# Group 1's channels with exchanged halves: x of both groups in eight 32x64 float32 tiles, weights summed on TensorE, own buffers for the last five stores

## The chip, the core and the metric

The kernel runs on one core of a Trainium2 chip. The metric is the device time of one launch in microseconds (us). The core has five engines that each work through their own list of instructions in order: TensorE (PE in the profile, PEld its weight loads), VectorE (DVE), ScalarE (ACT), GpSimd (POOL) and SyncE (SP), which here issues every DMA. They wait for each other through semaphores. TensorE writes into PSUM, a small memory of eight banks (512 float32 per partition each); all other tiles lie in SBUF.

## The reference

Two attentions and a gated convolution, in numpy, with B = 8 batches, H = 8 heads, S = 576 positions, D = 64, 32 packed queries, and 512 channels (H times D):

```python
def sm_attn(qq, kk, vv):
    s = scale * np.matmul(qq, kk.transpose(0, 1, 3, 2))
    s = s - np.max(s, axis=-1, keepdims=True)
    a = np.exp(s)
    a = a / (np.sum(a, axis=-1, keepdims=True) + 1e-09)
    return np.matmul(a, vv)
p_packed = sm_attn(p, k, v)                 # 32 rows per head
x = sm_attn(q, p_packed, p_packed)          # then heads side by side: B, S, 512
...
for k in range(K):                          # K = 5 taps, causal, per channel
    gate_pre += conv_w[k][None, None, :] * xp[:, k:k + S, :]
gate = 1.0 / (1.0 + np.exp(-gate_pre))
val = x @ w_val
return (gate * val @ w_out).astype(np.float32)
```

The three weights `w_val`, `conv_w` and `w_out` arrive as float64, all else as float32.

## The kernel before

The work is done batch by batch, with heads in two groups g of four (hl = 0 to 3; each has 32 rows of a 128-partition tile). Channels come in four chunks of 128, two per group, so a chunk is two heads.

A batch runs through these steps, each a generator with a letter. Loads K, V, Q, P. `keys` (k) and `queries` (q) turn the loaded tiles by TensorE transposes (tiles `kpt`, `qpt`) that ACT copies to `kT`, `qT`. `attn_pack` (a, lines 343 to 387) makes the first attention: scores `s`, maximum `nb` on DVE, exponential `a` on ACT, transposes `at`, products `pv`, and from these the packed values: `ppd` (each head's 64 values twice, ACT) and `pp` (the same with a mask of zeros, DVE). `packed_turned` (p) turns `ppd` into `ppT`. `attn_out` (s) and `weighted` (t) make the second attention's weights: scores, 32x32 transposes into `t` on DVE, subtraction and scaling on POOL, exponential on ACT, transposes into `a2`; then `a2h`, its rounding to float32r on ACT, and `a2l`, the rest, on DVE. Float32r takes one pass through TensorE, and a product of two split numbers takes three float32r matmuls. `packed_values` (w) multiplies the packed values with `w_val` (`wp`, split into `wph` and `wpl`), so that `value` (v, line 523) needs 12 float32r matmuls per chunk, of `a2h` and `a2l` with these (`val`).

`mixed` (x, line 463) makes x itself, for the convolution. The matrix of a pair of heads has 64 rows and 128 columns, half of them the mask's zeros; `pp` is split into `pph` (ACT) and `ppl` (POOL), and for each group and each half of the positions (288 columns) six float32r matmuls, three for each pair, fill one PSUM tile of two banks, one bank per pair. ACT copies it to `xp`. `gate` (g, line 503) does the five taps per chunk (one on ACT, four on DVE, tile `sig`) and a tanh on ACT. In `value`, DVE multiplies gate and value (`sig<-sig,val`), ACT rounds to `gvh`, POOL takes the rest `gvl`. `project` (o, line 576) multiplies these with `w_out` in 12 float32r matmuls of 512 columns per 128 positions; ACT copies the sum to `osb` (two buffers) and SP stores it. For the last batch five such sums (c = 4 to 8) are held in PSUM until the last chunk of values is there.

The weights come first, once: each tile of 128x512 float64 is loaded as pairs of 32-bit words (tile `words`, five buffers), turned into a float32 `top` and a small `rest` by bit operations (`from_double`, line 240), and added on POOL: to `wv` (W, line 267), `cw` (C), and, split in two, `woh` and `wol` (O, line 289).

The PSUM tiles of two banks have the tag `big`, with two buffers: scores of both attentions, `wp`, x, `val` and one of the last sums share them. The tag `mid` has three buffers of one bank, `out` one.

The order of everything is a table written out in the kernel (`ORDER`, line 49): each token, as `v3.2`, runs the generator `value` of batch 3 for two of its steps. Engines do what they are given in that order, each waiting for its own inputs. The tag of a tile in a name is followed by batch, group or chunk: `x_3_1_0` is batch 3, group 1, half 0, `val_2_3` batch 2, chunk 3. The program's instructions are all issued from a helper, so the profile shows line 94 for each of them; names tell them apart.

Of the kernel before, what the change touches and what calls it, by code (L numbers as in the profile page):

```python
# [9 lines left out]
F32 = mybir.dt.float32  # L10
# [18 lines left out]
 'pp': 2,  # L29
 'ppd': 1,  # L30
 'ppT': 2,
 'pph': 1,
 'ppl': 1,
# [21 lines left out]
q1 t0 q1 g0 t0 w1 O0 g0 q1.2 w1 O0 q1.2 s1 O0 k2 q1 O0 s1 q1 K2 k2.2 V2 O0 s1 q1 Q2 k2.2 V2 k2 Q2 s1 K3 a2 P4 O0
s1.2 a2 s1 a2 k2 g0 k2.2 s1 g0 t0 v0 k2 g0 s1 t1 k2 s1 x0 v0 t1 k2 k3 | v0 a2 g0 x0 q2 k3 a2 v0 x0 q2 t1 q2 a2.3
x0 g0 v0 a2 q2 g0 x1 t1 x1 a2 q2 a2 t1 a2 q2.2 g0 a2.2 q2 t1 g0 x1 q2 g0 x1 v0 t1 a2 k3 q2 a2 x1 K3 x1 a2 V3 k3
g0 k3 Q3 v0 q2 P5 t1 k3.2 v0 q2 a2 t1 v0 k3 g0 a2 x1 t1 a2.3 g0 k3 a2.2 k3 g0 k3 a2.2 g0 p2 a3 g0 v0 p2 g0 k3.2
s2 v0 a3 k3 k4 v0 s2 a3 q3 s2 a3 q3 V3 g0 Q3 v0 K4 k4 a3 s2 K4 P6 a3.2 g0 a3 q3 s2 w2 g0 a3 q3 t2 g0 x1 a3 q3
a3.2 w2 v0 t2 a3.2 w2 v0 s2 q3 v0 g1 t2 o0 a3.2 t2 a3 g1 t2 s2 v1 o0 g1 s2 a3 g1 q3 a3.2 s2 x1 q3 o0 a3 Q4 o0 V4  # L60
x1 g1 s2 g1 t2 g1 v1 a3 t2 o0 k4 a3.2 o0 v1 g1 x1 k4 V4 t2 a3 v1 p3 x1 v1 a3 p3 t2 g1 x2 s3 t2 g1 q3 k4 s3 x2
q3.2 k4 o0 g1 q3 Q4 s3 g1 x2 g1 s3 v1.2 g1 q4 s3 k4 v1 q4.2 o0 K5 s3 k4 o0 q4 g1 k4 a4 s3 k4.2 g1 v1 k4 s3 g1 o0
a4 s3 g1.2 v1 a4 g1 s3 g1 v1 x2 o0 q4 g1 x2.2 o0 v1 q4 Q5 q4 x2 v1 q4 g1.2 x2.2 t3 g2 k4 v1 t3 x2 q4 K5 k4 k5 x2
v1 P7 g2 a4 q4 t3 x2 v1 o1 k5 a4 t3 x3 g2 a4.2 x3 t3 a4 o1 k5 t3 a4.2 o1 v2 k5 a4 g2 t3 a4 o1 a4 g2 t3 g2.2 v2
t3 q4 g2 v2 k5 Q5 t3 a4 q4 k5 g2 k5 o1 V5 w3 a4.2 v2 o1 k5 a4 K6 a4 k5 g2 a4.2 w3 o1 g2 k5 w3 a4 x3 g2.3 v2 o1
g2 o1 g2 o1 v2 g2 v2 g2 v2 g2 v2 o1 g2 o1 k5 g2 a4 x3 k5 v2 a4.2 g2 x3.2 v2 g2 V5 k5 a4 x3 a4 p4 v2 a5 K6 k5 p4
v2 g2 a5 x3 g3 a5 g3 o1 v2 g3 v2 g3 a5 v2 o1 v3 o1 a5 g3 a5 o2 a5 g3.2 v3 g3 v3 g3 a5 o2 k6 s4 v3 a5 o2 k6 x3 s4
q5 x3 a5 g3 x3 q5 a5 v3 s4 x3 g3 x4 s4 g3 a5 q5 g3 v3 o2 x4 s4 x4 g3 a5 q5 v3 t4 v3 a5 o2 s4 o2 a5.2 t4 V6 a5.2
q5 s4 a5.2 v3 q5 Q6 g3 a5 t4 g3 q5 t4 a5 s4 k6 q5 a5 w4 g3 k6 t4 g3 q5 k6 s4 g3 v3 a5 k6 w4 g3 x4 V6 o2 v3 g3 s4
w4 v3 x4 a5 q5 a5 t4 p5 o2 k6 g3 p5 q5 o2 k6.2 q5 t4 x4 Q6 k6 K7 s5 x4 g3 k6 s5 v3 g3 x4 t4 g4 k6 s5 t4 a6 g4 k6  # L70
v3 s5 q6 k6 K7 o2 a6 q6 v3 g4 s5 t4 a6 g4 t5 a6 o2 s5 o2 v3 a6 o3 s5 a6 t5 a6 s5 g4 t5 s5 g4 v4 g4 s5 g4 a6 o3
# [39 lines left out]
def packed_attention_gated_conv(  # L111
# [69 lines left out]
    for hl in range(4):  # L181
        nc.gpsimd.memset(mask[heads[hl], hl % 2, :], 1.0)
# [31 lines left out]

    def words_of(nm, src, rows):
# [442 lines left out]
```

## Time and profile before

| what | us |
|---|---|
| median of 3 runs (lowest, highest) | 329.72 (329.62, 330.51) |
| the profiled execution's own time | 330.79 |
| its span, first to last instruction | 329.0 |
| PE busy | 287.6 |
| DVE busy | 259.0 |
| ACT busy | 215.3 |
| POOL busy | 123.2 |

An engine's busy time is the union of its instructions' times. Matmuls overlap in the array, so the pace of TensorE is read from one start to the next and not from durations: 12 matmuls of `o` take 2.75 us, though each lasts about 0.39. In a row of the timeline the columns are the start, the duration, the engine, the instruction, the tiles as out<-in, their shapes, and in brackets the idle time before it with what ended it; "x16" is sixteen records merged (a float32 matmul leaves two).

### The profile page before, as it was taken

Reading aid. Unit: us, or ns where it says so; the run is one execution under the profiler, and the core shown is the slowest. Engines: PE = TensorE matmul, PEld = TensorE weight load, DVE = VectorE, ACT = ScalarE, POOL = GpSimd, SP = SyncE. Lnnn points to the kernel's source line nnn. Section 1 sums busy time; section 2 is a strip of 40 time slices with the busy share of each in tenths; the row PEclk is TensorE's granted clock in tenths of the full one; section 3 lists DMA queues with packets and bytes.
Section 4 is the critical chain, followed back from the end, with each engine's and each line's share of the span. In section 5 each row is a group of like instructions: output and inputs, shape, how many; then the busy total and the mean of one; then the engine's idle time right before and its main releaser. Section 6 shows DMA issues by size and latency. Waiting matters only on the chain.

```text
span 329.0 us, 7252 instructions
## 1 busy us (share of the span) xinstructions
PE 287.6 (87%) x2932; PEld 220.6 (67%) x2932; DVE 259.0 (79%) x381; ACT 215.3 (65%) x440; POOL 123.2 (37%) x115
## 2 busy tenths in 40 slices
PE   0157987979989999999999898989999999999990
PEld 0134744657758877877877677776868868778870
DVE  0794288689999999997797999998997899776600
ACT  0347788779986779777686867776677755655201
POOL 1334536374153455323245434415431237323200
PEclk9999997699999999999999999999999999999996
DMA  7999989495895765383507491635011011211013
GB/s 197 232 255 263 257 162 239 108 230 108 211 217 135 187 166 136 90 241 92 157 34 173 118 237 37 175 87 126 32 66 34 32 35 38 70 53 64 34 24 135
DMA packets 42474, 43.47 MB, mean 132 GB/s; under 512 B 6085, under 2 KB 36805, under 8 KB 42442
## 3 DMA queue, kind: packets, MB, share of 16 engines
q1 hardware_dynamic: 42442, 43.02, 53.6%
q8 instruction: 23, 0.38, 0.5%
q14 instruction: 9, 0.07, 0.1%
HBM read 33.57 MB, written 9.44 MB: 131 GB/s over the span
## 4 chain that ended last, share of the span: by engine, by line
PE 40%; DVE 31%; ACT 17%; issue 4%; DMA 3%; POOL 3%; SPq 1%; ACTq 0%; POOLq 0%
DVE sig L94 16%; PE o L94 15%; PE val L94 8%; ACT sig L94 4%; DVE a2l L94 3%; PE x L94 3%; PE s L94 3%; PE kpt L94 3%; PE pv L94 2%; DVE sm L94 2%; PE at L94 2%; DVE t L94 2%; DVE nb L94 2%; DMA wv_words<-in_moe_w_val_dram 2%; PE qpt L94 2%
## 5 line engine op out<-in xcount | busy, mean ns | idle before, releaser
L94 DVE SCALAR_TENSOR_TENSOR sig<-xp,cw,sig 128x576 f32<-128x576 f32 x128 | 122.6, 958 | 11.6 <-ACT sig L94 10.1
L94 POOL TENSOR_TENSOR gvl<-sig,gvh 128x576 fp32r<-128x576 f32 x31 | 49.1, 1584 | 80.0 <-ACT gvh L94 77.0
L94 PE MATMUL o<-woh,gvh 128*128 128x512 f32 x144 | 58.6, 407 | 0.8 <-ACT osb L94 0.8
L94 PE MATMUL o<-woh,gvl 128*128 128x512 f32 x144 | 56.5, 392 | 0.1
L94 PE MATMUL o<-wol,gvh 128*128 128x512 f32 x144 | 56.5, 392 | 0.0
L94 PE MATMUL val<-a2h,wph 128*128 128x288 f32 x128 | 39.6, 309 | 0.5 <-ACT a L94 0.5
L94 PE MATMUL val<-a2l,wph 128*128 128x288 f32 x128 | 37.9, 296 | 0.9 <-DVE a2l L94 0.9
L94 ACT COPY osb<-o 128x512 f32<-128x512 f32 x34 | 19.8, 582 | 28.3 <-PE o L94 22.6
L94 PE MATMUL val<-a2h,wpl 128*128 128x288 f32 x128 | 37.9, 296 | 0.0
L94 PEld LDWEIGHTS o<-woh,gvh 128*128 128x128 f32 x144 | 27.0, 188 | 10.3 <-issue 2.3
L94 ACT CAST gvh<-sig 128x576 fp32r<-128x576 f32 x32 | 21.7, 678 | 17.7 <-DVE sig L94 17.6
L94 POOL TENSOR_TENSOR t<-t,mx 128x576 f32<-128x576 f32 x16 | 24.2, 1513 | 22.0 <-DVE mx L94 22.0
L94 PEld LDWEIGHTS o<-woh,gvl 128*128 128x128 f32 x144 | 27.1, 188 | 6.6 <-POOL gvl L94 0.5
L94 ACT ACTIVATE sig<-sig 128x576 f32<-128x576 f32 x32 | 21.9, 686 | 13.1 <-DVE sig L94 12.9
L94 PEld LDWEIGHTS o<-wol,gvh 128*128 128x128 f32 x144 | 27.1, 188 | 4.6
L94 POOL TENSOR_TENSOR t<-t,rs 128x576 f32<-128x576 f32 x16 | 20.0, 1248 | 23.0 <-DVE rs L94 15.8
L94 DVE SCALAR_TENSOR_TENSOR sig<-sig,val 128x576 f32<-128x576 f32 x32 | 23.7, 741 | 5.6 <-PE val L94 3.0
L94 PE MATMUL qpt<-ident,qm 96*128 96x96 f32 x192 | 26.1, 270 | 1.1 <-ACT kT L94 1.1
L94 PE MATMUL kpt<-ident,km 96*128 96x96 f32 x192 | 26.8, 276 | 0.1
L94 PEld LDWEIGHTS val<-a2h,wph 128*128 128x128 f32 x128 | 24.2, 189 | 3.6 <-ACT a L94 1.2
L94 PEld LDWEIGHTS qpt<-ident,qm 96*128 96x128 f32 x192 | 21.0, 155 | 7.3 <-issue 4.3
L94 PEld LDWEIGHTS kpt<-ident,km 96*128 96x128 f32 x192 | 20.9, 156 | 6.9 <-issue 4.7
(87 smaller groups left out, 561.8 us busy)
## 6 DMA issues: line engine op xcount, KB each, us to landing
km<-in_k_dram SPq DMA_DIRECT2D x16, 576.0 KB, 7.4
vm<-in_v_dram SPq DMA_DIRECT2D x16, 576.0 KB, 6.1
qm<-in_q_dram SPq DMA_DIRECT2D x16, 576.0 KB, 6.0
out_dram<-osb SPq DMA_DIRECT2D x24, 256.0 KB, 2.2
wv_words<-in_moe_w_val_dram SPq DMA_DIRECT2D x8, 256.0 KB, 7.2
wo_words<-in_moe_w_out_dram SPq DMA_DIRECT2D x4, 512.0 KB, 10.0
out_dram<-osb SPq DMA_DIRECT2D x8, 192.0 KB, 2.3
p<-in_p_dram SPq DMA_DIRECT2D x16, 64.0 KB, 9.0
```

Of the source, the lines that this page charges most:

```text
L94: made = getattr(self.engine, op)(*args, **kw)
```

## The change

**x (`mixed`).** `pp`, its mask, `pph` and `ppl` go. Each head is a tile of its own: 32 rows (its packed positions) by 64 columns (its channels), in plain float32, from `ppd` and `a2` directly. Both groups of a half are issued together, eight matmuls into two `big` tiles, and ACT copies the two afterwards. Head hl of group g writes partitions 0 to 63 or 64 to 127, by (hl + g) mod 2. In group 1 the two heads of a chunk therefore stand in exchanged halves, so that the eight tiles cover all four positions of 32 rows and both of 64 columns.

**Channels.** To match, the chunks of group 1 have exchanged halves everywhere: the loads of `w_out` and `conv_w` fetch them so, and `wv`'s columns are exchanged in the copy.

**Weights.** TensorE adds `top` and `rest`: two float32 matmuls with the identity into one PSUM bank (tag `mid`). `wv` is then copied by ACT in two pieces; `woh` is ACT's rounding of half of the sum, and `wol` one DVE operation on the sum. The `rest` of `w_out`, before an ACT and a POOL operation, is a DVE operation, as it was for `w_val`. For each tile of `w_out` POOL loses three operations, ACT two, and DVE has two more; for each of `w_val` POOL loses one and ACT has two more.

**Last stores.** The five last sums get buffers of their own: two of `osb`, two of `t2`'s, one of `a2`'s.

**Order.** The table is written anew.

```diff
+def summed(nm, words):
+    ps = one(f"{nm}_sum")
+    pe.matmul(ps, ident, st["top", nm], start=True, stop=False)
+    pe.matmul(ps, ident, words[:, :, 0].bitcast(F32), start=False, stop=True)
+    return ps
 def value_weights(b):
...
-            pool.tensor_tensor(
-                wv[:, c, :], st["top", f"wv{c}"], words[:, :, 0].bitcast(F32), op=ALU.add
-            )
+            ps = summed(f"wv{c}", words)
+            yield
+            for low in range(2):
+                cs = slice(low * DM // 2, low * DM // 2 + DM // 2)
+                to, x = (
+                    y[:, cs].rearrange("a (x t d) -> a x t d", x=2, t=2) for y in (wv[:, c], ps)
+                )
+                act.copy(to[:, :, ::-1] if low else to, x)
+                yield
 def out_weights(b):
...
-            yield from from_double(f"wo{c}", words, P, 0.5, True)
-            top, hi = st["top", f"wo{c}"], woh[:, c, :]
-            act.mul(top, top, 0.5)
-            yield
-            act.copy(hi, top)
-            yield
-            pool.tensor_tensor(top, top, hi.bitcast(F32), op=ALU.subtract)
-            yield
-            pool.tensor_tensor(wol[:, c, :], top, words[:, :, 0].bitcast(F32), op=ALU.add)
+            yield from from_double(f"wo{c}", words, P)
+            ps, hi = summed(f"wo{c}", words), woh[:, c, :]
+            yield
+            act.mul(hi, ps, 0.5)
+            yield
+            dve.scalar_tensor_tensor(
+                wol[:, c, :], ps, 0.5, hi.bitcast(F32), op0=ALU.mult, op1=ALU.subtract
+            )
             yield
 def attn_pack(b):
...
-            dve.scalar_tensor_tensor(pp[:, g], pv2, rs, mask, op0=ALU.mult, op1=ALU.mult)
 def mixed(b):
...
+        for half in range(2):
+            hc = slice(half * HS, half * HS + HS)
+            pp, a2 = st["ppd", b], st["a2", b]
+            xps = [big(f"x_{b}_{g}_{half}") for g in range(G)]
+            for g in range(G):
+                for hl in range(4):
+                    at = D * ((hl + g) % 2)
+                    pe.matmul(
+                        xps[g][at : at + D, hl // 2, :HS],
+                        pp[heads[hl], g, 0, :],
+                        a2[heads[hl], g, hc],
+                        start=True,
+                        stop=True,
+                    )
+            yield
+            for g in range(G):
+                act.copy(st["xp", b, g][:, :, half, PAD:], xps[g][:, :, :HS])
                 yield
 def project(b):
...
+            if b == B - 1 and c % 2:
+                osb = tile_of("t2", [P, G, NBLK, NP], F32, f"osb_{b}_{c}")
+                osb = osb.rearrange("a g y z -> a (g y z)")[:, :DM]
+            elif b == B - 1 and c == 8:
+                osb = tile_of("a2", [P, G, S], F32, f"osb_{b}_{c}")[:, 0, :DM]
+            else:
+                osb = tile_of("osb", [P, DM], F32, f"osb_{b}_{c}")
 ORDER (start)
-K0 L0.3 V0 P0 W0.13 L0 W0 L0 W0 L0 Q0 W0 K0 W0 k0 P1 W0 k0.4 W0 k0.2 W0 C0 W0 k0 C0 a0 W0 C0 W0 a0 W0 a0 q0 C0
+x0 K0 x0 L0 Q0 L0 P0 W0.9 q0 K0 W0 V0 q0.2 W0 V0 q0.2 Q0 W0 q0 L0 W0.2 L0 W0.2 L0 k0.11 a0 k0.2 a0 k0 a0.15 q0
```

How the table moves instructions shows at three places. TensorE at the program's start, before (`pTt` turns the packed queries, `qpt` and `kpt` a third of a group's queries or keys):

```order
L94 MATMUL pTt_0_131<-ident_64,p_0_97 128x128 x2
L94 MATMUL kpt_0_0_0_141<-ident_64,km_0_0_84 128x96 x4
L94 MATMUL kpt_0_0_1_147<-ident_64,km_0_0_84 128x96 x4
L94 MATMUL kpt_0_0_2_155<-ident_64,km_0_0_84 128x96 x4
L94 MATMUL s1_0_0_166<-kT_0_0_140,pT_0_138 32x288 x8
```

and now (`wv0_sum` and `wv1_sum` are the first two tiles of `w_val`):

```order
L89 MATMUL wv0_sum_101<-wv0_top_95,ident_64 128x512
L89 MATMUL wv0_sum_101<-wv0_words_84,ident_64 128x512
L89 MATMUL qpt_0_0_0_109<-ident_64,qm_0_0_87 128x96 x4
L89 MATMUL qpt_0_0_1_120<-ident_64,qm_0_0_87 128x96 x4
L89 MATMUL qpt_0_0_2_129<-ident_64,qm_0_0_87 128x96 x4
L89 MATMUL wv1_sum_142<-wv1_top_106,ident_64 128x512
L89 MATMUL wv1_sum_142<-wv1_words_89,ident_64 128x512
L89 MATMUL pTt_0_154<-ident_64,p_0_92 128x128 x2
```

Two sums and a third of the queries now stand ahead of the first transposes of keys and of `s1_0_0`, the first scores.

ScalarE at the program's start, before:

```order
L94 ACTIVATE wv0_top_100<-wv0_words_86 128x512
L94 ACTIVATE wv1_top_107<-wv1_words_89 128x512
L94 ACTIVATE wv2_top_114<-wv2_words_92 128x512
L94 ACTIVATE pT_0_138<-pTt_0_131 128x256
L94 COPY kT_0_0_140<-kpt_0_0_0_141 128x4x96
```

and now:

```order
L89 ACTIVATE wv0_top_95<-wv0_words_84 128x512
L89 COPY wv_71<-wv0_sum_101 128x256
L89 COPY wv_71<-wv0_sum_101 128x2x2x64
L89 ACTIVATE wv1_top_106<-wv1_words_89 128x512
L89 COPY qT_0_0_108<-qpt_0_0_0_109 128x4x96
```

The two copies of the first sum now stand ahead of `wv1_top`, the first step of the second tile.

TensorE around batch 3's x, before (first half, then what follows up to the second half's end):

```order
L94 MATMUL x_3_0_0_2047<-a2h_3_1727,pph_3_1796 128x288 x2
L94 MATMUL x_3_0_0_2047<-a2h_3_1727,ppl_3_1797 128x288 x2
L94 MATMUL x_3_0_0_2047<-a2l_3_1728,pph_3_1796 128x288 x2
L94 MATMUL pv_4_1_2057<-vm_4_1_1472,a1t_4_1_1941 32x64 x24
L94 MATMUL x_3_0_1_2084<-a2h_3_1727,pph_3_1796 128x288 x2
L94 MATMUL x_3_0_1_2084<-a2h_3_1727,ppl_3_1797 128x288 x2
L94 MATMUL x_3_0_1_2084<-a2l_3_1728,pph_3_1796 128x288 x2
```

and now, around the second half:

```order
L89 MATMUL val_2_3_2056<-a2h_2_1302,wph_2_1332 128x288
L89 MATMUL val_2_3_2056<-a2h_2_1302,wpl_2_1333 128x288
L89 MATMUL val_2_3_2056<-a2l_2_1303,wph_2_1332 128x288
L89 MATMUL x_3_0_1_2075<-a2_3_1822,ppd_3_1296 64x288 x4
L89 MATMUL x_3_1_1_2076<-a2_3_1822,ppd_3_1296 64x288 x4
L89 MATMUL ppTt_4_2086<-ident_64,ppd_4_1803 128x128 x2
```

The second half of both groups stands right behind the last matmuls of `val_2_3`, which fill the other `big` tile; the rows before have one group each, with other work between.

More of the change, by code (lines that the diff above doesn't have):

```diff
@@ L28 @@
  'pT': 1,
- 'pp': 2,
- 'ppd': 1,
+ 'ppd': 2,
  'ppT': 2,
- 'pph': 1,
- 'ppl': 1,
  'qT': 2,
@@ L55 @@
[L55 to L59, printed above, removed]
@@ L177, in packed_attention_gated_conv @@
     heads = [slice(NP * hl, NP * hl + NP) for hl in range(4)]
-    pairs = [slice(2 * NP * pr, 2 * NP * pr + 2 * NP) for pr in range(2)]
-    mask = const.tile([P, 2, D], F32, name="mask")
-    nc.gpsimd.memset(mask, 0.0)
-    for hl in range(4):
-        nc.gpsimd.memset(mask[heads[hl], hl % 2, :], 1.0)
     eps = const.tile([P, G * NBLK], F32, name="eps")
```

113 lines of the change are left out of this document (46 added, 67 removed).

## Prediction

> **What bounds the kernel now.** I read the page first: the engines' shares and the chain that ended last.
>
> ```profile
> span 329.0 us, 7252 instructions
> PE 287.6 (87%) x2932; PEld 220.6 (67%) x2932; DVE 259.0 (79%) x381; ACT 215.3 (65%) x440; POOL 123.2 (37%) x115
> PE 40%; DVE 31%; ACT 17%; issue 4%; DMA 3%; POOL 3%; SPq 1%; ACTq 0%; POOLq 0%
> ```
>
> TensorE is busy longest and DVE is second, and both are on the chain, so no single engine sets the time everywhere. The busy time by stretches tells where each does. Its columns are the stretch, its length, and the busy time of PE, PEld, DVE, ACT and POOL, each with its number of instructions; then the granted clock.
>
> ```profile
> core 0: us, PE busy (x) PEld busy (x) DVE busy (x) ACT busy (x) POOL busy (x), PEclk, DMA share, GB/s
> 0.00:44.00 44.00, 22.50 (x247) 15.36 (x248) 22.01 (x39) 21.19 (x45) 15.37 (x25) 1.00 1.04 240
> 44.00:72.00 28.00, 23.07 (x297) 14.88 (x298) 22.57 (x37) 22.98 (x51) 15.08 (x13) 0.82 0.84 176
> 72.00:100.00 28.00, 26.39 (x399) 19.52 (x398) 26.18 (x46) 25.47 (x58) 12.35 (x12) 1.00 0.86 182
> 100.00:180.00 80.00, 79.80 (x819) 63.22 (x818) 71.93 (x104) 57.91 (x122) 30.81 (x27) 1.00 0.53 140
> 180.00:260.00 80.00, 76.31 (x823) 58.99 (x822) 72.65 (x104) 58.62 (x118) 28.72 (x26) 1.00 0.39 100
> 260.00:307.00 47.00, 45.75 (x299) 37.62 (x298) 39.87 (x50) 26.05 (x45) 20.88 (x16) 1.00 0.14 46
> 321.00:329.00 8.00, 0.00 (x0) 0.00 (x0) 0.69 (x1) 1.17 (x2) 0.00 (x0) 0.65 0.37 132
> ```
>
> There are three parts. Up to 72 nothing is full: PE is idle for 21.5 of the first 44 us and for 4.9 of the next 28, DVE for 22.0 and 5.4, so the length of batch 0's chain counts. From 100 to 180 PE has no gap (79.80 of 80); from 180 to 307 PE and DVE are both near full, and wait for each other. In the last 8 us no matmul runs at all.
>
> **The change part by part.** *The last stores.* The timeline's end, with ACT's copies of the sums:
>
> ```profile
> 317.63 0.39 PE L94 MATMUL o<-woh,gvl 128*128 128x512 f32 x1
> ...
> 318.06 0.59 ACT L94 COPY osb<-o 128x512 f32<-128x512 f32 x1 [7.92 <-PE o L94]
> ...
> 320.35 0.39 PE L94 MATMUL o<-woh,gvl 128*128 128x512 f32 x1
> 321.72 0.58 ACT L94 COPY osb<-o 128x512 f32<-128x512 f32 x1 [3.07 <-DMA out_dram<-osb]
> ...
> 324.83 0.59 ACT L94 COPY osb<-o 128x512 f32<-128x512 f32 x1 [2.53 <-DMA out_dram<-osb]
> ```
>
> The first sum ends at 317.63 + 0.39 = 318.02 and is copied 0.04 later. The last ends at 320.74, but its copy waits for a store to free one of two buffers and starts at 324.83. With five buffers it starts at 320.78: **-4.0**. What is late next is the last matmul itself; the stores stay in line on SP, but each is short. This gain needs only that PE's end stays where it is relative to the rest.
>
> *x on TensorE.* One half of one group, six float32r matmuls, and behind it a set of eight float32 score tiles (64 rows by 32 columns each, 288 positions, side by side in the array):
>
> ```profile
> 238.37 0.40 PE L94 MATMUL x<-a2h,pph 64*128 64x288 f32 x2
> ...
> 238.96 0.72 PE L94 MATMUL s<-kT,pT 64*32 64x288 f32 x16
> ...
> 239.61 0.55 PE L94 MATMUL kpt<-ident,km 96*128 96x96 f32 x4
> ```
>
> From start to start, x's half takes 238.96 - 238.37 = 0.59 and the scores' set 0.65. The new half of both groups is also eight float32 tiles of 288 positions, only of another shape; I take the scores' 0.65. If the eight didn't run side by side at all, each would take about a set's time, 8 x 0.65 = 5.2; below 0.65 I see no way, since as many positions stream through. In batches 1 to 7 PE then does 14 x 0.65 = 9.1 in place of 28 x 0.59 = 16.5: 7.4 less.
>
> *What x took on the other engines.*
>
> ```profile
> L94 DVE SCALAR_TENSOR_TENSOR pp<-pv,sm,mask 128x128 f32<-128x128 f32 x16 | 5.4, 338 | 7.3 <-ACT ppd L94 7.2
> L94 POOL TENSOR_TENSOR ppl<-pp,pph 128x256 fp32r<-128x256 f32 x8 | 7.1, 894 | 5.5 <-ACT pph L94 4.6 <-POOL gvl L94 0.9
> L94 DVE SCALAR_TENSOR_TENSOR sig<-xp,cw,sig 128x576 f32<-128x576 f32 x128 | 122.6, 958 | 11.6 <-ACT sig L94 10.1
> L94 DVE SCALAR_TENSOR_TENSOR sig<-xp,cw,sig x128: 718/818/2069, 58.7 to 307.1; 128x576 f32<-128x576 f32 x128
> ```
>
> DVE loses `pp`, 14 x 0.338 = 4.7 in batches 1 to 7. It also loses collisions with POOL: the gate's operation has a median of 818 ns, a mean of 958 and up to 2069, an excess of 128 x 0.14 = 17.9 us over POOL's 123.2 busy us, or 0.145 per us of POOL; `ppl`'s 7.1 are worth 1.0. DVE has 5.7 less. Where PE and DVE wait for each other, I count the smaller of 7.4 and 5.7: **-5.7** (between -7.4 and 0, if the new order leaves the room as gaps).
>
> *Two big buffers at once.* x now fills both `big` buffers, so it waits for the reader of the tile filled just before, not of the one before that. PE is in order: everything behind x waits too. The readers:
>
> ```profile
> L94 DVE SCALAR_TENSOR_TENSOR sig<-sig,val 128x576 f32<-128x576 f32 x32 | 23.7, 741 | 5.6 <-PE val L94 3.0 <-ACT sig L94 2.3
> L94 ACT COPY xp<-x 128x576 f32<-128x576 f32 x32 | 20.6, 644 | 2.8 <-PE x L94 2.5
> L94 ACT CAST wph<-wp 128x1024 fp32r<-128x1024 f32 x8 | 8.1, 1013 | 2.2 <-PE wp L94 2.2
> L94 DVE TENSOR_TENSOR wpl<-wp,wph 128x1024 fp32r<-128x1024 f32 x8 | 9.8, 1220 | 1.9 <-ACT wph L94 1.8
> ```
>
> In the new order eight of the 14 halves of batches 1 to 7 have under 1 us of PE work between the tile filled last and themselves. Four have 0.2 or none: two right behind a `val` chunk (batch 3, as quoted, and batch 7: 0.74 to wait each), one behind `wp_5` (1.01 + 1.22 - 0.2 = 2.0), one behind its own first half in batch 6 (2 x 0.644 - 0.2 = 1.1); a fifth, in batch 1, has 0.7 against such copies (0.6). That is 5.2; I take two thirds, **+3.5**, since PE isn't the late one at each. It is nothing where PE would have waited anyway, and 14 x 1.29 = 18 if every half waited for two copies; the others have 0.7 to 3 us of transposes, products or `o` as cover.
>
> *The weights.* A sum is two float32 matmuls of 512 columns. Nearest is the set of eight float32 `wp` matmuls of 512 columns, side by side:
>
> ```profile
> 41.38 1.96 PE L94 MATMUL wp<-wv,ppT 64*32 64x512 f32 x16
> 141.20 1.09 PE L94 MATMUL wp<-wv,ppT 64*32 64x512 f32 x16
> 142.22 0.42 PE L94 MATMUL at<-ident,a 128*96 128x128 f32 x2
> L94 PE MATMUL o<-woh,gvl 128*128 128x512 f32 x144 | 56.5, 392 | 0.1
> L94 DVE SCALAR_TENSOR_TENSOR wv_top<-wv_top,wv_words 128x512 uint32<-128x512 uint32 x4 | 5.5, 1378 | 0.3
> L94 DVE SCALAR_TENSOR_TENSOR wo_top<-wo_top,wo_words 128x512 uint32<-128x512 uint32 x4 | 2.7, 674 | 0.1
> ```
>
> The set takes 1.02 from start to start at 141 and 1.96 at 41; one matmul alone can't take longer, nor less than a float32r pass (0.392). I take 0.9, so 1.8 a sum and 14.4 for eight (6.3 to 31). Three (w_val's) fall into the first 44 us, where PE's 21.5 idle cover them; five, 9.0, come in 44 to 100, where PE is idle for 4.9 + 1.6: 2.5 stay uncovered. DVE gets eight operations more, 8 x 0.674 = 5.4, under its 5.4 + 1.8 idle in the same stretch. POOL's additions of w_val go, beside which `wv_top` took 1378 ns in place of 674: 4 x 0.70 = 2.8 less on DVE, of which I count 1.0, since DVE often waits there. Opening: **+1.5**. The first product `val`, which came at 69.62,
>
> ```profile
> 69.62 0.40 PE L94 MATMUL val<-a2h,wph 128*128 128x288 f32 x1 [0.49 <-ACT a L94]
> ```
>
> now stands behind fewer instructions, but transposes of batch 2 that were ahead of it come behind it: moved, not saved, and I count nothing. ACT's changes (`pph` gone, eight small copies more) lie in its idle time, 9 to 45% of each stretch from 44 on.
>
> The sum: -4.0 - 5.7 + 3.5 + 1.5 = -4.7. The profiled execution took 330.79, 1.8 more than its span of 329.0, and 1.1 more than the median of 329.72; -4.7 makes its span 324.3 and the median **325.0**. A difference of 0.3%, 1.0 us, is about the least that a measurement here can tell.
>
> **The rivals.** *A: tiles that share a bank (slower).* In the present kernel, whatever runs side by side on different rows writes to different PSUM banks: the pairs of x, the halves of the scores, the groups of `wp`. In the new x, heads 0 and 1 (and 2 and 3) of a group sit on different rows and write one bank, though other partitions. If such tiles took turns, a half would take two rounds, 1.3, and PE 16 x 0.65 = 10.4 more: 325.0 + 10.4 = 335.4. It decides the sign from 0.65 + 4.7/16 = 0.94 a half. No row here shows two row tiles in one bank, for or against; the different partitions speak against it. Chance 0.12. The Trainium skill, TensorEngine Tiling (Array Packing), section Gotcha 1: PSUM Pressure, says that "Different row tiles cannot access same PSUM bank simultaneously"; by that rule the time is this rival's.
>
> *B: the opening comes later (slower).* ACT takes `wv1_top` only after the first sum and its copies, and PE turns the first keys only after two sums.
>
> ```profile
> 9.91 0.69 ACT L94 ACTIVATE wv_top<-wv_words 128x512 f32<-128x512 f32 x1 [0.28 <-DMA wv_words<-in_moe_w_val_dram]
> 15.10 0.66 PE L94 MATMUL pTt<-ident,p 128*128 128x128 f32 x2 [15.10 <-DMA p<-in_p_dram]
> 21.04 1.22 PE L94 MATMUL s<-kT,pT 64*32 64x288 f32 x16 [3.36 <-ACT kT L94]
> ```
>
> With sums of 3.9 and copies of some 0.4, `wv1_top` moves from 9.91 to about 16.7, and the first scores, behind the second sum, from 21.04 to about 27.7: +6.7, if nothing of it is won back by the shorter way from there: 331.7. For it: `pTt` at 15.10 had been waiting for a load. Against: PE's idle 21.5. Chance 0.13.
>
> *C: the opening comes sooner.*
>
> ```profile
> 26.31 2.18 PE L94 MATMUL kpt<-ident,km 96*128 96x96 f32 x12
> 65.47 1.06 PE L94 MATMUL kpt<-ident,km 96*128 96x96 f32 x8
> ```
>
> At 26 a transpose takes 0.18, at 65 0.13, and the `wp` set took 1.96 at 41: early PE works at a slower pace, though the granted clock reads 1.00. If the long sums bring the full pace from 16 us on, PE's 22.5 busy us in the first 44 shrink by up to half, 11; about half of this would lie on batch 0's chain: -6, so 319. Chance 0.17. The Trainium skill, TensorE: Matmul & The Clock Gate, Part 1, says that the array runs at half clock until about 3.4 us of sustained activity; by that rule a first sum is nearly enough, and the pace in these rows agrees, the granted clock doesn't.
>
> *D: only the stores.* DVE's count of operations stays (-5.4 `pp`, +5.4 weights), and if DVE's order sets the middle, PE's room becomes gaps: 329.72 - 4.0 = 325.7. For it: PE 76.31 of 80 beside DVE 72.65. Chance 0.10.
>
> **How the numbers follow.** My forecast has 0.48. Faster by over 0.3% (below 328.7): 0.85 of it, C, 0.8 of D: 0.66, rounded to 0.65. Slower (above 330.7): A, 0.8 of B and a little of the forecast's own spread: 0.25. Within: 0.10. The range takes in B and C and leaves A out, with 1.5 beyond both for the unknown sums and waits: 317.5 to 333.
>
> **What would show it.** Right: the last `osb` copy within 0.1 of PE's end; x's eight tiles at 0.6 to 0.7 a half; sums at about 1.8; PE's gaps from 100 on grown by waits of `x` for ACT or DVE of some 3.5 in all. Rival A shows as a half of 1.3, B and C in the time of the first scores and of the first `val`, D as PE gaps in the middle with DVE full. The forecast is wrong if the time from the first `val` to PE's end doesn't shrink, beyond the work moved behind it.

## The result, and the profile after

The changed kernel takes 354.56 us (median of 4 runs, 353.1 to 355.63), the kernel before 329.74 beside it: ratio 1.0745, 95% interval 1.0692 to 1.0797. It is slower by 7%; the forecast was 325.0, and the time lies far outside its range. The profiled execution took 353.1 us. One execution each of e4, e7 and e18 below fell into a slower state; the medians count them, the ratios don't.

The page of the changed kernel, the span and the engines' shares:

```profile
span 351.3 us, 7407 instructions
PE 297.6 (85%) x3028; PEld 212.8 (61%) x3028; DVE 257.8 (73%) x373; ACT 210.4 (60%) x432; POOL 96.0 (27%) x86
```

TensorE is busy for 10.0 us more than before, and 53.7 us of the span are without it, before 41.4. So of the span's 22.3 us, 10.0 are more work (or slower work) and 12.3 are more waiting. To see where, I cut both executions at the same places: the first product times gate of batch 1, the last of batch 7, TensorE's end. The kernel before:

```profile
0.00:107.35 107.35, 79.31 (x984) 56.02 (x985) 77.82 (x133) 74.00 (x161) 44.46 (x49) 0.95 0.91 201
107.35:308.68 201.33, 196.19 (x1898) 154.95 (x1897) 178.27 (x247) 138.92 (x276) 78.75 (x66) 1.00 0.38 102
308.68:320.74 12.06, 12.06 (x54) 9.63 (x52) 2.20 (x3) 1.26 (x2) 0.00 (x0) 1.00 0.07 16
```

The changed kernel:

```profile
0.00:107.96 107.96, 80.61 (x930) 49.25 (x931) 72.27 (x122) 64.42 (x144) 17.93 (x24) 0.94 0.90 186
107.96:337.48 229.52, 208.90 (x2065) 157.20 (x2064) 182.65 (x249) 143.51 (x284) 78.08 (x62) 0.99 0.37 96
337.48:345.55 8.07, 8.07 (x36) 6.33 (x34) 2.85 (x4) 1.85 (x3) 0.00 (x0) 1.00 0.10 24
```

The opening ends at the same time (+0.6), the last products are 4.0 shorter, and the tail behind TensorE's end goes from 8.26 to 5.75 (-2.5). The loss is in the middle: 201.33 becomes 229.52, +28.2. There TensorE has 12.7 us more work and 15.5 us more idle time (20.6 after 5.1). The opening did 54 records less, although it has the 32 records of the sums in it, and the last stretch 18 less (54 becomes 36, the 4.0 us above): what both leave is done in the middle.

What TensorE waits for in that middle, longest first (in all, times, longest):

```profile
PE o L89 <- ACT osb L89: 8.8, 9, 1.9
PE x L89 <- DVE a L89: 2.0, 1, 2.0
PE x L89 <- ACT xp L89: 2.0, 2, 1.1
PE x L89 <- DVE sig L89: 1.4, 4, 0.5
PE at L89 <- ACT ppd L89: 1.3, 1, 1.3
```

The waits before x are 5.4 in all, before 1.2. Of these, 3.4 are for the readers of the big tiles (`xp`, `sig`), which is what the forecast had for "two big buffers at once"; 2.0 are for x's own input, `a2`. The largest wait is another one, for ScalarE's copies of the sums `o`, which was 0.8 before.

What the forecast had foreseen in the small, in the timeline of the changed kernel:

```profile
20.52 1.67 PE L89 MATMUL kpt<-ident,km 96*128 96x96 f32 x16 [0.19 <-ACT wv L89]
...
32.54 1.12 PE L89 MATMUL wv_sum<-wv_top,ident 128*128 128x512 f32 x2
33.50 1.06 PE L89 MATMUL wv_sum<-wv_words,ident 128*128 128x512 f32 x2
34.49 0.71 PE L89 MATMUL s<-qT,ppT 64*32 64x288 f32 x16
...
56.74 0.38 PE L89 MATMUL val<-a2h,wph 128*128 128x288 f32 x1
...
128.48 0.71 PE L89 MATMUL x<-a,ppd 32*64 32x288 f32 x8
129.71 0.71 PE L89 MATMUL x<-a,ppd 32*64 32x288 f32 x8 [0.51 <-DVE sig L89]
130.35 0.55 PE L89 MATMUL kpt<-ident,km 96*128 96x96 f32 x4
...
133.02 0.74 PE L89 MATMUL x<-a,ppd 32*64 32x288 f32 x16
133.69 0.50 PE L89 MATMUL o<-woh,gvh 128*128 128x512 f32 x1
...
345.16 0.39 PE L89 MATMUL o<-woh,gvl 128*128 128x512 f32 x1
```

```profile
345.59 0.59 ACT L89 COPY osb<-o 128x512 f32<-128x512 f32 x1 [0.77 <-PE o L89]
```

A transpose of keys takes 0.10 at 20 us (before 0.18 at 26), so TensorE is at its full pace early. A sum takes 34.49 - 32.54 = 1.95 (1.8 was taken), and the last copy starts 0.04 after the last matmul ends. A half of x takes 0.67 at 133.02 (0.65 was taken). But of the 14 halves of batches 1 to 7 only three run like that, those at 93.19, 133.02 and 204.15. In six, as at 128.48, group 1 stands apart from group 0, mostly behind a wait for its big tile, and takes 0.64 of its own; five others take 0.8 to 1.5. Added up from start to start, without the waits, x of batches 1 to 7 takes some 15 us of TensorE (an estimate from these rows), where the forecast has 9.1 and the kernel before 16.5.

Two things looked like the cause. The first is what I call the hand-over: ScalarE's first tap of a batch comes late behind the last tanh of the batch before. In the kernel before, at batch 3, and in the changed kernel, at batch 4:

```profile
155.86 0.70 ACT L94 ACTIVATE sig<-sig 128x576 f32<-128x576 f32 x1
156.44 0.79 ACT L94 ACTIVATE sig<-xp,cw 128x576 f32<-128x576 f32 x1
```

```profile
194.89 0.68 ACT L89 ACTIVATE sig<-sig 128x576 f32<-128x576 f32 x1 [2.22 <-DVE sig L89]
...
206.02 0.79 ACT L89 ACTIVATE sig<-xp,cw 128x576 f32<-128x576 f32 x1
```

It was 0.58 there and is 11.13 here, from start to start; over the seven batches 7.7 became 54.9. With x of both groups made at once and two `xp` buffers, group 1's must be free before either group is copied, so x of a batch waits for the last tap of the one before (theory H). The rivals: x's tiles or the two big buffers (X, T), the sums on TensorE (W), the new order by itself (O).

### The profile page after: what moved, and what is told of

It is laid out like the page before. It is cut to its first block, busy times and chain, and to the rows that moved or that the text cites. A ratio compares the mean times of both kernels' runs of the same rounds, so it can differ in the third digit from the quotient of the medians.

```text
span 351.3 us, 7407 instructions
## 1 busy us (share of the span) xinstructions
PE 297.6 (85%) x3028; PEld 212.8 (61%) x3028; DVE 257.8 (73%) x373; ACT 210.4 (60%) x432; POOL 96.0 (27%) x86
## 4 chain that ended last, share of the span: by engine, by line
DVE 40%; PE 30%; ACT 15%; DMA 7%; issue 3%; SPq 2%; POOL 1%; DVEq 0%; POOLq 0%; ACTq 0%
DVE sig L89 25%; PE o L89 11%; DMA wv_words<-in_moe_w_val_dram 6%; ACT sig L89 5%; PE val L89 5%; DVE sm L89 3%; PE x L89 3%; PE kpt L89 3%; DVE wpl L89 2%; DVE mx L89 2%; DVE t L89 2%; SPq L89 2%; DVE a L89 2%; ACT xp L89 2%; DMA wo_words<-in_moe_w_out_dram 2%
## 5 line engine op out<-in xcount | busy, mean ns | idle before, releaser
L89 DVE SCALAR_TENSOR_TENSOR sig<-xp,cw,sig 128x576 f32<-128x576 f32 x128 | 124.1, 970 | 25.7 <-ACT sig L89 23.2
L89 PE MATMUL o<-woh,gvh 128*128 128x512 f32 x144 | 59.5, 414 | 8.8 <-ACT osb L89 8.8
L89 PEld LDWEIGHTS o<-woh,gvh 128*128 128x128 f32 x144 | 27.3, 190 | 21.9 <-ACT osb L89 12.9
L89 PE MATMUL val<-a2h,wpl 128*128 128x288 f32 x128 | 37.7, 295 | 0.0
L89 ACT COPY osb<-o 128x512 f32<-128x512 f32 x34 | 19.8, 581 | 20.6 <-PE o L89 17.4
L89 PE MATMUL kpt<-ident,km 96*128 96x96 f32 x192 | 25.0, 260 | 5.6 <-ACT kT L89 4.3
L89 POOL TENSOR_TENSOR t<-t,rs 128x576 f32<-128x576 f32 x16 | 21.2, 1324 | 31.1 <-DVE rs L89 26.8
L89 ACT CAST gvh<-sig 128x576 fp32r<-128x576 f32 x32 | 21.6, 674 | 10.2 <-DVE sig L89 8.0
L89 PEld LDWEIGHTS kpt<-ident,km 96*128 96x128 f32 x192 | 19.6, 146 | 11.1 <-ACT kT L89 5.0
L89 ACT COPY kT<-kpt 128x384 f32<-128x384 f32 x48 | 22.7, 487 | 5.4 <-PE kpt L89 5.4
L89 PE MATMUL qpt<-ident,qm 96*128 96x96 f32 x192 | 24.4, 252 | 1.0 <-ACT a1t L89 0.7
```

The lines of the kernel that those rows point to most:

```text
L89: made = getattr(self.engine, op)(*args, **kw)
```

## The experiments

All ratios are to the kernel before, with 95% intervals.

**e1, the five store buffers alone.**

```diff
+            if b == B - 1 and c % 2:
+                osb = tile_of("t2", [P, G, NBLK, NP], F32, f"osb_{b}_{c}")
...
+            elif b == B - 1 and c == 8:
+                osb = tile_of("a2", [P, G, S], F32, f"osb_{b}_{c}")[:, 0, :DM]
```

> The kernel before with one edit: the last five sums get store buffers of their own. The prediction's term: 4.0 us less, 325.7, with the last copy to osb within 0.1 us of the last matmul; the stores then end within about 2 us of each other. A rival: the stores themselves queue up behind each other and little is won, 328 to 329.7.

328.34 us, 0.9947 (0.9925 to 0.997). The last copy starts at TensorE's end:

```profile
321.16 0.39 PE L94 MATMUL o<-woh,gvl 128*128 128x512 f32 x1
```

```profile
321.59 0.58 ACT L94 COPY osb<-o 128x512 f32<-128x512 f32 x1 [0.77 <-PE o L94]
```

From TensorE's end to the span's end 5.65 us (327.2 - 321.55), before 8.26: 2.6 are won, not 4.0. The last store lands 5.0 us behind the end of the last copy (327.2 - 322.17), before 3.6 (329.0 - 325.42): the stores now stand in line.

**e2, the new x alone, by group, in the old order; e8, that and e1.**

```diff
-            dve.scalar_tensor_tensor(pp[:, g], pv2, rs, mask, op0=ALU.mult, op1=ALU.mult)
...
+                for hl in range(4):
+                    at = D * (hl % 2)
+                    pe.matmul(
+                        xps[at : at + D, hl // 2, :HS],
+                        pp[heads[hl], g, 0, :],
+                        a2[g][heads[hl], hc],
```

> The kernel before, its order kept step for step, with only the contents of x changed: float32 tiles of 32 by 64 from ppd and a2, one group at a time (four tiles a half, so 28 halves in batches 1 to 7), pp, pph, ppl gone; a2 has three buffers of one group each, ppd three. Theory H (the hand-over: what costs is that x of both groups of a batch waits for the previous batch's last tap, so that ScalarE's first tap comes some 7 us later at each of seven batches): no join here, so no loss; TensorE has 28 x 0.06 = 1.7 us more, DVE 5.7 less: 325 to 331. Rival X (the new x itself is dear, by its tiles or what waits for them): 340 or more. With H the time from the last tanh of a batch to ScalarE's first tap of the next stays at 0.6 to 3 us.

> The order of before with the new x by group and the five store buffers, and the weights left as they were: the two parts that were faster alone, by 3 us (e2) and 2.5 (e1). If they add up: 323 to 326, faster than both kernels. If the tail's gain needs the end that it had in e1: 327.

e2: 327.03, 0.9917 (0.9886 to 0.9947). e8: 324.78, 0.9831 (0.9803 to 0.986), faster than both kernels, and almost what was forecast for the change; that the number agrees is luck, since e8 has neither the joined x nor the sums. Four tiles take as long as eight at best:

```profile
236.08 0.71 PE L91 MATMUL x<-a,ppd 32*64 32x288 f32 x8
236.73 0.72 PE L91 MATMUL s<-kT,pT 64*32 64x288 f32 x16
```

0.65 from start to start. X falls: the new x is a gain, and it needs neither the join nor the new order. These kernels, and all below with x by group in the old order, hold `a2` in three tiles of one group and `ppd` in three, where the changed kernel has one `a2` tile for both groups and two of `ppd`.

**e3, all of the change but the join, the exchanged halves and the order.** e2's and e1's diffs and the sums:

```diff
+            ps = summed(f"wv{c}", words)
+            act.copy(wv[:, c, :], ps)
```

> Everything of the change but the join and the new table: the order of before, x in float32 by group, the weights' sums on TensorE, the five store buffers. Theory H: no loss, and the tail's 4 us are won: 318 to 329. Rival W (the weights' sums on TensorE are what costs): 340 or more. Rival X (the new x itself): 340 or more too, and then e2 shows it as well.

338.16, 1.0231 (1.0192 to 1.027), 13.4 above e8, from which it differs in the sums alone. In the old order the sums stand ahead of the first keys and wait there for the weights' tiles:

```profile
23.50 1.77 PE L91 MATMUL wv_sum<-wv_top,ident 128*128 128x512 f32 x2 [2.37 <-DVE wv_top L91]
25.06 1.91 PE L91 MATMUL wv_sum<-wv_words,ident 128*128 128x512 f32 x2
26.77 0.70 PE L91 MATMUL kpt<-ident,km 96*128 96x96 f32 x4
```

In e8 the first keys are turned at 15.90. This is the forecast's rival B, in the old order; the new order avoids it. So W holds here, for 13.4 us, and e11 asks it again in the new order.

**e4 and e7, the joined x in the old order, with a third `xp` buffer.** The contents are the changed kernel's; in the table, of batch 3 (x's matmuls and copies, for e4, then for e7):

```diff
+... w3 o1 g2 x3.2 k5 w3 x3.6 a4 g2.3 v2 ...
+... w3 a4 g2.3 v2 o1 g2 o1 g2 o1 v2 x3 g2 v2 g2 v2 g2 x3.2 v2 o1 g2 o1 k5 g2 a4 k5 v2 x3 a4.2 g2 v2 g2 x3.2 ...
```

> Everything of the change with the join (both groups' x at once, into both big buffers), but in the order of before, and with a third xp buffer, so that x only waits for the previous batch's second chunk and can be made while chunks 2 and 3 are gated; in batches 4 and 7 it comes at the previous gate's end because the weights a2 aren't ready before. Theory H: most of the loss is gone, 320 to 335, and the hand-over (last tanh to first tap) is under 3 us in batches 1, 2, 3, 5 and 6. Rival T (the two big buffers taken at once are what costs, wherever x stands): 345 or more, with TensorE's waits before x of over 10 us in all.

> As e4 (the joined x, three xp buffers, the order of before), but x stands behind a2h and a2l, and other work stands between its matmuls and its copies, so that ScalarE doesn't hold a2h back behind them. In e4 the a2l of batch 1 waited 2.98 us for a2h, which stood behind four copies. From the first val to the last it took 253.0 us in e4 and 234.5 in e3 without the join. If that queue on ScalarE was e4's loss: 238 to 246, so 341 to 350 in all, with the loss left in batches 4 and 7, whose x comes late. If taking both big buffers at once costs wherever it stands (T): 250 or more from the first val to the last.

e4: 363.25, 1.0979 (1.091 to 1.1048). e7: 357.17, 1.0799 (1.0768 to 1.083). From the first product to the last e4 takes 253.0 and e7 248.9, e3 234.5. e7 missed its 238 to 246. Of its 14.4 over e3, 10.9 arise at two steps, from batch 3 to 4 (17.0 for 11.0) and from 6 to 7 (10.6 for 5.7), where x comes late; the hand-over is 12.5 and 8.9 there and 0.6 to 3.3 elsewhere. e4 landed where the rival T had it (345 or more) and not where H did, though with 8.3 us of waits before x where T had over 10; by e7's steps, both big buffers at once cost little where x is early, and that spoke for H. The single `a2` tile came with the join in both, and was not tried apart.

**e6, the kernel before with group 0's x made late.** Only the table, here for batch 7:

```diff
-... v6 t7 v6 x7 g6 o5 x7.2 t7 v6 o5.2 g6 t7 x7.2 t7 g7 x7 g7 ...
+... v6 t7 v6 g6 o5 t7 v6 o5.2 g6 x7.4 t7 x7 t7 g7 x7 g7 ...
```

> The kernel before with nothing but its table altered: group 0's x of batches 1 to 7 (two halves, two copies) is moved behind the previous batch's last tanh, where the changed kernel has it; the work itself is as before. Theory H: 7 hand-overs of matmul, copy, matmul, copy, some 3 us each, so 15 to 25 us slower: 345 to 355. The rivals, for which x's place is no matter: 329 to 334.

351.47, 1.0643 (1.0604 to 1.0681): +21, with nothing altered but where x and a few steps of the gates around it stand. The hand-overs grow from 7.7 to 34.6. In the old order, H's price is real.

**e5 and e9, x by group in the changed kernel's order; e9 with the gate one chunk sooner too.** In the table, batch 3, changed, e5, e9:

```diff
-... v2 p4 k5 x3 v2 a5 p4 v2 x3 o2 a5 g3 k5 g3 ...
+... v2 p4 k5 v2 a5 p4 v2 o2 a5 g3 x3 k5 g3 x3 ...
+... q4 x3 g3 t3 a4 o1 t3 a4 q4 o1 a4.2 g3 q4.2 ...
```

> The changed kernel with its own order and everything else of it, but x one group at a time: group 0's two halves (four tiles each) stand in the order as soon as group 0's a2 is there, while chunks 2 and 3 of the previous batch are gated, and group 1's follow the previous batch's last tap, behind the first taps of group 0. TensorE has 14 sets of 0.65 us more, 9 us. Theory H (the hand-over: both groups' x waits for the previous batch's last tap): 333 to 345, the time from a batch's last tanh to ScalarE's next first tap under 3 us at most batches. Rivals T (two big buffers at once; here one group still takes both), W (weights' sums) and O (the new table, apart from x): 352 or more.

> As e5 (the changed kernel, its own order, x by group), with one more edit of the table: each batch's gate starts one chunk sooner, its first chunk's taps and tanh right behind the previous batch's last tanh and group 0's x, and every later chunk in the place of the one before. In e5 ScalarE's first tap still stood 27 to 42 steps behind the previous tanh in the order, and the hand-over stayed at 1.2 to 10.5 us, so that e5 did not undo what it should. Theory H: the hand-over falls to 1 to 4 us and the time to 332 to 345. Rivals T, W and O (the new table is slow for another reason): 352 or more.

e5: 362.42, 1.0941 (1.089 to 1.0992). e9: 370.34, 1.1227 (1.1157 to 1.1297). Both miss what H said. e5 didn't close the hand-over (1.2 to 10.5 us), as ScalarE's first tap had kept its place; e9 closed it at batches 1, 2 and 6 (0.6 to 1.6), and won nothing there. Against H, but with more work for TensorE in both.

**e13, e14 and e17, x left out in batches 1 to 7** (the gate reads batch 0's): of the changed kernel, of the kernel before, and of the changed kernel with the gate one chunk sooner.

```diff
+        if b:
+            for g in range(G):
+                st["xp", b, g] = st["xp", 0, g]
...
+            return
```

> The changed kernel with x left out in batches 1 to 7: no memset, no matmuls, no copies; the gate of those batches reads batch 0's x. The order is otherwise as it is. TensorE loses 14 halves of 0.67, 9.4 us, ScalarE 28 copies. Theory H (the gate waits for an x that comes late): the hand-over goes with it, and the time comes near that of the kernel before with the same left out (e14): within 10 us of it, 315 to 330. Rival O (the order is slow for other reasons): it stays 18 us or more above e14, at 335 or more.

> The kernel before with x left out in batches 1 to 7 in the same way (pph and ppl too); the gate reads batch 0's x. TensorE loses 16.5 us, ScalarE some 20, POOL 7. TensorE is full from 100 to 180 and nearly full behind it: 312 to 322 by every theory.

> As e13 (the changed kernel without x in batches 1 to 7), with each batch's gate one chunk sooner in the order: the first chunk's taps right behind the previous batch's last tanh, where nothing holds them any more. Theory G (what costs in the new order is that the gate starts late, whatever it waits for): the hand-over falls under 2 us and the time from e13's 342.0 towards e14's 324.5: 322 to 332. If the gate's place isn't it, and the work that the opening left behind and the sums are: 338 to 345.

e13: 342.03, 1.0349 (1.0301 to 1.0398). e14: 324.45, 0.9799 (0.9752 to 0.9846). e17: 344.44, 1.0439 (1.0407 to 1.0472). e14 missed its 312 to 322: taking 16.5 us of x off TensorE, and all that x costs the others, wins 6.4 us beside 330.8. Without any x the changed kernel stays 17.6 us above the old one (with x 24.8). The middle, from batch 1's first product to batch 7's last, of e14 and of e13:

```profile
106.94:303.76 196.82, 183.06 (x1742) 146.12 (x1741) 175.55 (x247) 124.12 (x245) 74.28 (x48) 0.98 0.39 104
```

```profile
108.12:328.13 220.01, 200.27 (x1875) 156.16 (x1874) 183.12 (x250) 130.38 (x260) 76.85 (x50) 0.97 0.40 101
```

It is 23.2 longer with no x, no join and no `a2` held by x, after 28.2 with them; 17.2 of it is work moved in from both ends, 6.0 is waiting. In e13 the hand-overs still sum to 38.5, as the first tap stands where it stood; in e17 nothing holds the gate:

```profile
183.36 0.69 ACT L89 ACTIVATE sig<-sig 128x576 f32<-128x576 f32 x1 [3.00 <-DVE sig L89]
183.95 0.76 ACT L89 ACTIVATE sig<-xp,cw 128x576 f32<-128x576 f32 x1
```

The hand-over is 0.59 at each of the seven batches, and the time is no better than e13's. So H falls as the main cause in the new order: what the hand-over leaves free there, other waits take (ScalarE's for `gvh`'s input, 11.1 in e13, is 17.9 in e17).

**e10, e12, e11 and e15, the two orders cut at the bar and put together crosswise.** e10 is the changed kernel up to the bar and the old order behind it (x by group); e12 is e10 with the weights added on POOL; e11 is the changed kernel with them on POOL; e15 is the old opening with the new order behind it, weights on POOL.

```diff
-            ps = summed(f"wv{c}", words)
...
+                pool.tensor_tensor(to[:, :, ::-1] if low else to, x, r, op=ALU.add)
```

> The changed kernel's order and contents up to the point where the weights are all in (the bar in the table), and behind it the order of before, with x by group in float32 (a2 three buffers of one group, ppd three) and the five store buffers. Theory H: the whole loss arises behind the bar, so 315 to 326, at or below e8, with the first val at about 63 as in the changed kernel. Rival W (the weights' sums cost 13 us here as in e3): 335 or more. If the early start only moves work (nothing of it kept): 323 to 328.

> e10 with the weights added as before, on POOL: the changed kernel's opening order, the order of before behind the bar, x by group, five store buffers. It differs from e8 in the opening's order alone and from e10 in the sums alone. If the sums' price is all that e10 has over e8 (324.8): 322 to 327. If the changed opening is itself slower than the old one without the sums, which bring TensorE to its full pace early: 329 to 336.

> The changed kernel with its order, but the weights added as before: w_val's on POOL (in two pieces, for the exchanged halves), w_out's on POOL and ScalarE, no sums on TensorE (the last two steps of w_out stand just ahead of the bar). If the eight sums' 15 us of TensorE's time are paid in full here as in e3 (13.4 against e8) and e10 (11.9): 340 to 345. If TensorE has room for them in this order, since it waits for other things anyway: 351 to 357.

> The reverse of e12: the order of before up to the bar, with the weights added on POOL, and behind it the changed kernel's own order with the joined x and two xp buffers; five store buffers; no sums on TensorE. If the loss sits in the order behind the bar, join and hand-over (18 us by the changed kernel against e10): e8's 324.8 + 18, 338 to 348. If most of it sits in the opening: 324 to 332.

e10: 336.55, 1.0201 (1.0153 to 1.0248). e12: 336.48, 1.0181 (1.0138 to 1.0223). e11: 358.07, 1.085 (1.0797 to 1.0903). e15: 367.21, 1.1104 (1.1054 to 1.1154). e10 falls where W had it (335 or more), but e12 is as slow without the sums, so it isn't theirs; e15 missed its 338 to 348. With the weights on POOL, the float32 x and the five stores throughout:

| us | old order behind the bar | new order behind the bar |
|---|---|---|
| old opening | 324.8 (e8) | 367.2 (e15) |
| new opening | 336.5 (e12) | 358.1 (e11) |

The new order behind the bar costs 42 or 22 us, the new opening 12 or less than nothing (e12 and e15 have a seam that nobody fitted). The right column has the joined x and one `a2` tile too, so the table alone doesn't part these from the order. The lengths of the middle do more:

| middle, us | runs |
|---|---|
| 199.1 to 199.4, old order, x by group | e8, e3, e10, e12 |
| 213.1 and 215.8, old order, joined x | e7, e4 |
| 228.5 to 231.2, new order, joined x | e11, changed kernel, e15 |
| 234.6, new order, x by group | e5 |

In the old order the middle is as long behind either opening, with the sums or without. In the new order it is 29 us or more longer behind either opening, with the join or without. The join with its one `a2` tile adds 13.7 and 16.5 in the old order (e7 and e4 after e3); in the new order x by group (e5) is no better. In the new opening the sums cost nothing: e10 is e12, and the changed kernel (354.6) isn't slower than e11. The middle of e10 beside that of the changed kernel above:

```profile
118.20:317.33 199.13, 196.36 (x1948) 149.44 (x1948) 174.56 (x238) 137.45 (x270) 73.74 (x60) 1.00 0.40 103
```

The same batches take 199.13 in place of 229.52; TensorE waits for 2.8 us in place of 20.6, and has 117 records fewer to do. Its opening does 99 records more and ends 10.2 later (118.20 after 107.96), and what is behind the middle is 3.8 longer. So the moved work, 12.5 us less in the middle, comes back at the two ends, and what e10 wins is about TensorE's waiting: 17.8 us less, of 16.4 us in all between the two spans (351.3 and 334.9).

**e16, the new order with the old contents** (and the five stores; x of both groups at once, as six float32r matmuls each):

```diff
+            xps = [big(f"x_{b}_{g}_{half}") for g in range(G)]
+            for g in range(G):
+                for n, (w, x) in enumerate(((pph, ah), (ppl, ah), (pph, al))):
```

> The contents of before (pp, pph, ppl, six float32r matmuls a group and half, the weights added on POOL, natural channels; only the five store buffers are new) in the changed kernel's order, both groups' x at once where it has them (a few steps later, since this x needs a2h and a2l). TensorE has 7.4 us more for x than the changed kernel and no sums. If the order alone is the loss: 352 to 366. If the loss needs the new contents: 330 to 342.

373.40, 1.1317 (1.1275 to 1.1358); e1, the same with the old order, is 328.34. The order alone, with its join, takes 45 us. That is more than the 352 to 366 expected: with the contents that it was written for it does better than with any others tried that make x. Of the 45, 38.5 are in the middle (239.8 after 201.4), where this x reads `a2h` and `a2l` and doesn't hold `a2`; 10.4 are in the opening, and the end gives 4.2 back.

**e18, two banks for the sums o, in place of one.**

```diff
-PSB = {'big': 2, 'mid': 3, 'out': 1}
+PSB = {'big': 2, 'mid': 2, 'out': 2}
```

> The changed kernel with the PSUM banks split otherwise: two for the sums o and two for transposes and products (before one and three). TensorE then need not wait for ScalarE's copy of one sum before it begins the next. If these 8.8 us set the end: 345 to 350. If the waits are only where a lateness from elsewhere shows, or the lost bank makes as many waits for the transposes' copies: 352 to 362.

376.71, 1.1388 (1.1351 to 1.1425), beyond both ranges. The wait for `osb` is gone from the list, and others stand in it:

```profile
PE x L89 <- DVE a L89: 4.3, 1, 4.3
PE at L89 <- ACT qT L89: 3.6, 3, 1.7
PE at L89 <- ACT a1t L89: 3.0, 2, 2.7
PE at L89 <- ACT kT L89: 2.9, 4, 1.9
```

The lost third bank of transposes costs more than the wait for the sums. So the run doesn't tell whether that wait set the end.

**What stays open.** The new table is the loss. By steps, x by group and the store buffers win 5.0 us (e8), the new opening costs 11.8 (e10 over e8), and the new order behind the bar, with its join, 18.0 (the changed kernel over e10). The loss is there with the old contents (e16), with x by group (e5) and without x (e13). Neither the hand-over (e17) nor the sums (e11, e12) explain it, and no single trait of the order was found that does. How much the join and the one `a2` tile add within the new order was not tried apart. ScalarE's longest wait in the changed kernel's middle, and the same wait in e10's, where two others are longer:

```profile
ACT sig L89 <- DVE sig L89: 34.1, 20, 3.7
```

```profile
ACT sig L91 <- DVE sig L91: 10.8, 11, 1.9
```

TensorE's waits are mostly for copies that ScalarE makes. That these come late because ScalarE stands in front of a tanh, waiting for DVE's taps, is a reading of the trace, and was not tried apart.

## Why the prediction was wrong, point by point

**Where it failed.** The step is the sum's second term: "Where PE and DVE wait for each other, I count the smaller of 7.4 and 5.7: -5.7 (between -7.4 and 0, if the new order leaves the room as gaps)". The worst that the new table could do was set to nothing. It was looked at in three places (the opening, x's neighbours, the end) and taken as neutral between them, though "The table is written anew" was part of the change. In the middle TensorE has 15.5 us more waiting and 12.7 us more work, 4.0 of it from the end and most of the rest from the opening: +28.2 for a term that could be 0 at worst. None of the rivals had that either; D had gaps of TensorE, but with DVE full, and DVE is busy for 182.65 of the 229.52, a smaller share than before (178.27 of 201.33). The term's size was wrong too: its 7.4 us less of TensorE for x came to about 1, by the rows of the 14 halves, and in the old order e14 wins only 6.4 us with all of x gone.

**x's size.** Right for a half whose two big tiles are free, 0.67, and wrong for most: 3 of 14 ran so, and x took some 15 us in place of 9.1. The forecast took "the scores' 0.65" for each half and counted the wait for the second tile, but not that four tiles apart take as long as eight. Rival A falls as a mechanism: it needed 1.3 where the row at 133.02 shows 0.67, and e2's four tiles, two to a bank, take 0.65. The gain of the new x is real in the old order (e2: 0.9917, 2.7 us less). By the row of x at 133.02 eight tiles on four row positions, two of them in one bank on other partitions, run side by side. The Trainium skill, TensorEngine Tiling (Array Packing), section Gotcha 1: PSUM Pressure, says that they can't; the measurement decides, and disagrees.

**The tail.** Right in mechanism, 0.04 from TensorE's end to the last copy; in size 2.5 and 2.6 in place of 4.0, since the stores queue behind the copies. "What is late next is the last matmul itself" left out the stores' own line.

**Two big buffers.** 3.4 us of waits for the big tiles, for the +3.5 forecast: right in size, as far as the waits go. They are small beside the rest.

**The weights.** 1.95 a sum, where TensorE is at pace. The price wasn't 1.5 but depends on where the sums stand: 13.4 in the old opening (e3 against e8), none in the new (e10 against e12).

**The opening.** The first `val` came at 56.74, before at 69.62, and the sentence "moved, not saved, and I count nothing" was right about the first half: the opening up to batch 1's first product is as long as before. It was wrong to count nothing, since what was moved behind it came to where TensorE is full: beside e8, with the same middle, e10's opening costs 11.8, for the +1.5 forecast. Rival B is what e3 shows in the old order; in the changed kernel the first scores come at 22.12, before at 21.04, so it didn't come about there. Rival C's fast pace came (0.10 a transpose), and its 6 us did not: the opening up to batch 1 is no shorter.

**The test that the prediction named** ("the forecast is wrong if the time from the first `val` to PE's end doesn't shrink") came out against it: 345.55 - 56.74 = 288.8, before 320.74 - 69.62 = 251.1. The test goes on "beyond the work moved behind it"; the first `val` stands 12.9 us earlier, and that is a third of the 37.7.

## What to carry to other kernels

A table that orders every instruction is part of the kernel's contents: when it is written anew, price it by itself, by what each engine has left undone at a few fixed points and by the in-order queues between them, and never take it as neutral. Change the contents in the old order first (e8 is faster than both kernels), and the order alone after that (e16). A wait that is long in the trace may be only where a lateness shows: the hand-over was 55 us long, and closing it without x (e17) gave nothing.

## What the runs showed of the hardware

In the opening of the changed kernel TensorE waits for 4.33 us, from 37.81 on, and its granted clock falls to half:

```profile
42.14 0.90 PE L89 MATMUL kpt<-ident,km 96*128 96x96 f32 x4 [4.33 <-ACT kT L89]
...
44.81 1.97 PE L89 MATMUL wv_sum<-wv_top,ident 128*128 128x512 f32 x2
46.57 1.92 PE L89 MATMUL wv_sum<-wv_words,ident 128*128 128x512 f32 x2
48.41 0.84 PE L89 MATMUL x<-a,ppd 32*64 32x288 f32 x16
```

```profile
38.00:40.00 2.00, 0.00 (x0) 0.00 (x0) 1.24 (x4) 0.00 (x0) 1.54 (x2) 0.61 1.10 225
46.00:48.00 2.00, 2.00 (x3) 0.56 (x2) 1.73 (x4) 1.19 (x2) 0.00 (x0) 0.50 1.05 190
48.00:50.00 2.00, 1.73 (x21) 0.69 (x20) 1.09 (x3) 1.68 (x6) 0.00 (x0) 0.83 1.07 200
```

The grant is third from the end. A mean of 0.61 from 38 to 40 puts its fall from 1.00 to 0.50 at about 38.4, some 0.6 us into the wait. It is still 0.50 from 46 to 48, and the mean of 0.83 from 48 to 50 puts its return at about 48.7, 6.5 us after work is back at 42.14. The fourth sum of `w_val` takes 48.41 - 44.81 = 3.60 where the third took 1.95. So this gap cost more than its length. The Trainium skill, TensorE: Matmul & The Clock Gate, Part 1, has the clock at half after an idle window of about 3.4 us; these rows don't show that, since the grant is at half long before 3.4 us of this wait have passed, and the measurement decides. The stretch up to batch 1's first product, in e10 with the sums and in e12 without:

```profile
0.00:118.20 118.20, 88.95 (x1029) 54.91 (x1030) 75.51 (x133) 70.87 (x159) 20.61 (x26) 0.91 0.86 183
```

```profile
0.00:118.69 118.69, 83.80 (x997) 56.96 (x998) 75.68 (x125) 74.17 (x159) 44.38 (x46) 0.84 0.86 181
```

Without the sums the mean grant is 0.84, with them 0.91, and the stretch is as long. That the sums keep the clock up and so pay for themselves fits this, and was not tried apart.
